# One PSUM tile for each running sum in the gated part, in place of one tile for two

## The chip, the cores and the metric

The kernel runs on one core of a Trainium2 chip. The metric is the device time in microseconds (us) of one execution. The kernel before took 1139.19 us, the median of three runs (1138.51 to 1140.39). One execution was recorded by the profiler; its own time was 1137.8 us, of which the profile shows a span of 1136.0 us.

## The reference

```python
# attention inside chunks of 64 tokens, 8 heads of 64
scores = matmul(q_c, k_c.T) / sqrt(64); attn = softmax(scores); out = matmul(attn, v_c)
x = out as (8*576, 512)
# feed-forward
xn = (x - mean) / sqrt(var + 1e-6) * g_ln
x2 = x + maximum(xn @ w_ch1, 0) @ w_ch2          # 512 -> 2048 -> 512
# gated convolution
gate = sigmoid(causal 5-tap convolution of x2 along the sequence, per channel)
result = (gate * (x2 @ w_val)) @ w_out            # 512 -> 512 -> 512
```

The last line, with its two products of 512x512 weights, is what this text calls the gated part.

## The kernel before

The 4608 tokens are handled as nine blocks of 512. Blocks pass through attention, the feed-forward and the convolution one after the other; the gates of each block and seven prepared operands of its x2 (`x7_dram`) are kept in DRAM. The gated part comes last. For each block it runs a set of seven products for x2 @ w_val (`val`, line 1419) and a set of seven for the product with w_out (`proj`, line 1541). It is the seven-product scheme for 2x2 quadrants, so each product works on quadrants of 256x256. A product is twelve matmuls of 128x256 (`twelve`, line 881, which records all of them at line 888), since each number is carried as a high and a low part.

The seven products carry the names "1" to "7" and add up in two running sums in PSUM, called "a" and "b". Of a set, products 1, 6, 7 and 4 go into a, one upon the other. Products 5 and 3 go into b, and product 2 starts b anew, before 5 in `val` and after 3 in `proj`. Between two products of one sum the sum is read: `shot` (lines 1466 to 1471 in `val`, 1569 to 1573 in `proj`) copies it with ScalarE into SBUF, and `two` (line 1478) or `join` (line 1577) adds it with VectorE to an earlier copy. By these readings the four quadrants arise: c11 from products 1 and 2, c12 from 6 and 3, c22 from 5 and 7, c21 from 4. A product may start only when the reading that its sum is due has been made; so 6 waits for the shot s1 of 1, 7 for the shot u2 of 6, 3 for the shot s5 of 5, and 4 for the join c22 that follows 7.

In `val` the quadrants are multiplied by the gates and split into high and low parts (`split`, tiles `gv`, lines 1489 and 1493), which are the operands of `proj`.

PSUM has eight banks of 128x512 floats. The kernel allocates them under tags: `h0` and `h1` are single banks, `pr`, `yA` and `yB` pairs of banks. A pair is one tile of two banks. Before the gated part `h0`, `h1` hold hidden sums, `yA`, `yB` the feed-forward's results, `pr` the attention. In the gated part the function `banks` (line 1412) hands out the two sums of a set: for `val` of even blocks both banks of `pr` as one tile, for odd blocks `h0` and `h1` as two tiles; for `proj` both banks of `yA` for even and both of `yB` for odd blocks, as one tile each.

The order of the instructions on every engine is made by a list scheduler in the kernel (`Plan.run`, line 53). Each step is an op with an engine, an assumed duration, a list of ops that it depends on, and a priority; `take(tag)` and `hold(tag, ...)` state which earlier ops a room must wait for. The scheduler plays the ops through with its assumed durations and emits them in that order. The semaphore waits are not the scheduler's: the tile layer puts them in afterwards, from the tiles that each emitted instruction reads and writes. Instructions of one engine run in the order in which they were emitted. All DMAs are issued from SP's queue.

Of the kernel before, what the change touches and what calls it, by code (L numbers as in the profile page):

```python
# [31 lines left out]
class Plan:  # L32
# [8 lines left out]
    def add(self, eng, dur, fn, deps=(), pri=0.0):  # L41
        op = Op(eng if isinstance(eng, tuple) else (eng,), dur, fn, deps, pri, len(self.ops))
        self.ops.append(op)
        return op

    def take(self, tag):

        return self.held.get(tag, [])

    def hold(self, tag, *ops):  # L50
        self.held[tag] = list(ops)
# [55 lines left out]
def chunk_attention_ffn_gated_conv(  # L107
# [83 lines left out]
    def bank(tag, name):  # L191
        return psum.tile([P, 512], F32, tag=tag, name=name)

    def pair(tag, name):
        return psum.tile([P, 2, 512], F32, tag=tag, name=name)

    plan = Plan()
    add, take, hold = plan.add, plan.take, plan.hold
# [1206 lines left out]
    def sig_room(i):  # L1405
        if i < 4:
            return qk_room[:, i * 512 : (i + 1) * 512]
        return sums["f32"][:, i - 4]

    V_ORDER, P_ORDER = "2165374", "1657432"  # L1410

    def banks(tag, i):

        if tag == "h":
            return [bank(f"h{x}", f"gp{i}_{x}").rearrange("p (f x) -> p f x", f=2) for x in range(2)]
        t = pair(tag, f"gp{i}")
        return [t[:, x].rearrange("p (f x) -> p f x", f=2) for x in range(2)]

    def val(jj):
        j = TURN[jj]  # L1420
        pri = B0 + SET * jj
        pt = ("pr", "h")[jj % 2]
        pt_free = take("h0") + take("h1") + take("gh") if pt == "h" else take("pr")
        st, xr, sig, sg_op = {}, {}, {}, {}

        def gate(i, kh, h):
            room = 4 * (jj % 2) + i

            def load():
                sig[kh, h] = t = sig_room(room).rearrange("p (k x) -> p k x", k=2)  # L1430
                nc.sync.dma_start(
                    out=t, in_=gate_dram[j][:, 2 * kh : 2 * kh + 2, NB // 2 * h : NB // 2 * (h + 1)]
                )

            def sigmoid():
                nc.scalar.activation(out=sig[kh, h], in_=sig[kh, h], func=AF.Sigmoid)

            stores = [conv_store[j, f] for f in (2 * kh, 2 * kh + 1)]
            first = take("qk") + take("u2") + take("u3") if jj == 0 else []
            ld = add("SP", 1300, load, stores + take(f"sg{room}") + first, pri - SET)  # L1440
            sg_op[kh, h] = add("ACT", 640, sigmoid, [ld, sig_ok], pri - SET / 4)
            return f"sg{room}"

        rooms = {q: gate(i, *q) for i, q in enumerate(((0, 0), (0, 1), (1, 1), (1, 0)))}

        def product(m, into, new, deps):
            rt = X2_RING[x2_n[0] % len(X2_RING)]
            x2_n[0] += 1

            def load():  # L1450
                t = operand(rt[1]) if rt[0] == "o" else slot(rt, [P, 2, 2, 2 * P], F32R, f"x7_{j}_{m}r")
                xr[m] = lambda s, k: t[:, s, k]
                nc.sync.dma_start(out=t.bitcast(F32), in_=x7_dram[j, m].bitcast(F32))

            def go():
                if not st:
                    st["a"], st["b"] = banks(pt, f"v{j}")
                twelve(st[into], wv[m], xr[m], new)

            at = pri + 2 * M_TIME * V_ORDER.index(m)  # L1460
            ld = add("SP", 1300, load, [x7_store[j, m]] + take(rt), at - 30000.0)
            o = add("PE", M_TIME, go, [ld] + wv_op[m] + deps, at)
            hold(rt, o)
            return o

        def shot(into, tag, *deps):
            def go():
                st[tag] = slot(tag, [P, 2, 2 * P], F32, f"v{j}_{tag}")
                nc.scalar.activation(out=st[tag], in_=st[into], func=AF.Copy)

            return add("ACT", 620, go, list(deps) + take(tag), pri - 1e7)

        def two(tag, x, y, op, *deps, rank=-1e7):
            def go():
                if tag not in st:
                    st[tag] = slot(tag, [P, 2, 2 * P], F32, f"v{j}_{tag}")
                a, c = (sig[z] if isinstance(z, tuple) else st[z] for z in (x, y))
                nc.vector.tensor_tensor(out=st[tag], in0=a, in1=c, op=op)

            return add("DVE", 700, go, deps, pri + rank)  # L1480

        def split(m, tag, *deps):
            rt = GV_RING[gv_n[0] % len(GV_RING)]
            gv_n[0] += 1

            def high():
                st[m] = t = slot(rt, [P, 2, 2, 2 * P], F32R, f"gv{j}_{m}")
                gv_o[j, m] = lambda s, k: t[:, s, k]
                nc.scalar.activation(out=t[:, 0], in_=st[tag], func=AF.Copy)

            def low():
                t = st[m]
                nc.vector.tensor_tensor(out=t[:, 1], in0=st[tag], in1=t[:, 0].bitcast(F32), op=ALU.subtract)

            oh = add("ACT", 640, high, list(deps) + take(rt), pri)
            gv_op[j, m] = ol = add("DVE", 700, low, [oh], pri)
            gv_room[j, m] = rt
            return ol

        MUL, ADD, SUB = ALU.mult, ALU.add, ALU.subtract  # L1500
        m2 = product("2", "b", True, pt_free)
        m1 = product("1", "a", True, pt_free)
        s1 = shot("a", "hh0", m1)
        c11 = two("hh0", "hh0", "b", ADD, s1, m2)
        m6 = product("6", "a", False, [m1, s1])
        m5 = product("5", "b", True, [c11])
        u2 = shot("a", "hh1", m6)
        s5 = shot("b", "hl0", m5)
        m3 = product("3", "b", False, [m5, s5])
        m7 = product("7", "a", False, [m6, u2])  # L1510
        c12 = two("hh1", "hh1", "b", ADD, u2, m3)
        c22 = two("hl0", "hl0", "a", ADD, s5, m7)
        m4 = product("4", "a", False, [m7, c22])
        g11 = two("hh0", "hh0", (0, 0), MUL, c11, sg_op[0, 0], rank=-1e5)
        g12 = two("hh1", "hh1", (0, 1), MUL, c12, sg_op[0, 1], rank=-1e5)
        g22 = two("hl0", "hl0", (1, 1), MUL, c22, sg_op[1, 1], rank=-1e5)
        g21 = two("P", "a", (1, 0), MUL, m4, sg_op[1, 0], *take("P"))
        for q, o in (((0, 0), g11), ((0, 1), g12), ((1, 1), g22), ((1, 0), g21)):
            hold(rooms[q], o)
        if pt == "h":  # L1520
            hold("gh", g21, c12)
        else:
            hold("pr", g21, c12)

        l1 = split("1", "hh0", g11)
        s3 = two("hh1", "hh0", "hh1", SUB, g11, g12, rank=0)
        l7 = split("7", "hh1", s3)
        l4 = split("4", "hl0", g22)
        s2 = two("hl0", "hl0", "hh1", SUB, l4, g22, s3, rank=0)
        l6 = split("6", "hl0", s2)  # L1530
        s1_ = two("hh0", "hl0", "hh0", ADD, l1, s2, s3, rank=0)
        l5 = split("5", "hh0", s1_)
        l2 = split("2", "P", g21)
        s4 = two("P", "P", "hl0", SUB, l2, g21, s2, rank=0)
        l3 = split("3", "P", s4)
        hold("hh0", l5)
        hold("hh1", l7, s2)
        hold("hl0", l6, s4, s1_)
        hold("P", l3)

    def proj(jj):
        j = TURN[jj]
        pri = B0 + SET * (jj + 1) + 5 * M_TIME
        pt = f"y{'AB'[jj % 2]}"
        st = {}

        def product(m, into, new, deps):
            def go():
                if "a" not in st:
                    st["a"], st["b"] = banks(pt, f"o{j}")  # L1550
                twelve(st[into], gv_o[j, m], wo[m], new)

            at = pri + 2 * M_TIME * P_ORDER.index(m)
            o = add("PE", M_TIME, go, [gv_op[j, m]] + wo_op[m] + deps, at)
            hold(gv_room[j, m], o)
            return o
# [31 lines left out]
            hold(rooms[h], add("SP", 1300, go, deps, pri))  # L1588

        room0, room1 = (take(r) for r in rooms)  # L1590
        m1 = product("1", "a", True, take(pt))
        s1 = shot("a", 0, 0, m1, *room0)
        m6 = product("6", "a", False, [m1, s1])
        m5 = product("5", "b", True, take(pt))
        u2 = shot("a", 0, 1, m6, *room0)
        s5 = shot("b", 1, 1, m5, *room1)
        m7 = product("7", "a", False, [m6, u2])
# [2 lines left out]
        c21 = shot("a", 1, 0, m4, *room1)  # L1600
        store(1, c21, c22)
        m3 = product("3", "b", False, [m5, s5])
        c12 = join("b", 0, 1, m3, u2)
        m2 = product("2", "b", True, [c12])
        c11 = join("b", 0, 0, m2, s1)
        hold(pt, c21, c11)
        store(0, c11, c12)


# [72 lines left out]
```

## Time and profile before

| what | value |
|---|---|
| median of three runs | 1139.19 us |
| the profiled execution's own time | 1137.8 us |
| its span in the profile | 1136.0 us |
| TensorE matmul busy, over the span | 1092.4 us (96%) |
| TensorE weight loads busy, over the span | 957.0 us (84%) |
| VectorE, ScalarE busy, over the span | 865.3 us (76%), 497.9 us (44%) |
| first product of the gated part | at 921.1 us |
| last matmul ends | at 1130.3 us |

PE stands for TensorE's matmuls, PEld for its weight loads, which run ahead of the matmuls that use them; each matmul has one weight load of its own. DVE is VectorE, ACT ScalarE, SP the queue that issues DMAs. In the trace the `val` sums are `gpv` and the `proj` sums `gpo`; `os` is the SBUF tile that `proj` fills for the output. A number in square brackets at the end of a row of the timeline is the idle time of the engine just before the row, with what ended it.

### The profile page before, as it was taken

Reading aid. Unit: us, or ns where it says so; the run is one execution under the profiler, and the core shown is the slowest. Engines: PE = TensorE matmul, PEld = TensorE weight load, DVE = VectorE, ACT = ScalarE, POOL = GpSimd, SP = SyncE. Lnnn points to the kernel's source line nnn. Section 1 sums busy time; section 2 is a strip of 40 time slices with the busy share of each in tenths; the row PEclk is TensorE's granted clock in tenths of the full one; section 3 lists DMA queues with packets and bytes.
Section 4 is the critical chain, followed back from the end, with each engine's and each line's share of the span. In section 5 each row is a group of like instructions: output and inputs, shape, how many; then the busy total and the mean of one; then the engine's idle time right before and its main releaser. Section 6 shows DMA issues by size and latency. Waiting matters only on the chain.

```text
span 1136.0 us, 22506 instructions
## 1 busy us (share of the span) xinstructions
PE 1092.4 (96%) x8801; PEld 957.0 (84%) x8801; DVE 865.3 (76%) x1537; ACT 497.9 (44%) x893; POOL 29.1 (3%) x78
## 2 busy tenths in 40 slices
PE   5799999999999999999999999999999999999996
PEld 3478888788888888988888888889888888999995
DVE  5889969997867867876786596677748888887654
ACT  5885522334333334433433343343344546554542
POOL 0000000000000000000000000000000000000000
PEclk9889999999999999999999999999999999999999
DMA  9994334765988898888888779789948968999822
GB/s 208 333 290 116 84 98 134 249 211 175 308 255 224 254 328 286 267 296 253 226 276 292 216 219 318 211 228 304 274 147 289 390 235 281 305 316 362 300 77 74
DMA packets 178034, 275.72 MB, mean 243 GB/s; under 512 B 72196, under 2 KB 123400, under 8 KB 177928
## 3 DMA queue, kind: packets, MB, share of 16 engines
q1 hardware_dynamic: 177928, 274.29, 75.8%
q8 instruction: 69, 1.13, 0.4%
q14 instruction: 37, 0.30, 0.1%
HBM read 206.59 MB, written 67.63 MB: 241 GB/s over the span
## 4 chain that ended last, share of the span: by engine, by line
PE 87%; DVE 5%; DMA 3%; SPq 2%; ACT 1%; issue 1%; DVEq 0%; ACTq 0%
PE m L888 23%; PE gpv L888 7%; PE gpo L888 6%; PE yB L1044 5%; PE yA L1044 4%; PE yA L1045 4%; PE yA L1046 4%; PE yB L1045 4%; PE yB L1046 4%; PE att L478 4%; PE att L505 4%; PE h L726 3%; PE y L749 3%; PE h L727 3%; PE h L728 3%; PE y L751 3%
## 5 line engine op out<-in xcount | busy, mean ns | idle before, releaser
L888 PEld LDWEIGHTS m<-late,a 128*128 128x128 f32 x2352 | 298.9, 188 | 18.0 <-ACT c_hl L979 2.0
L888 PE MATMUL m<-late,a 128*128 128x256 f32 x2352 | 308.1, 282 | 3.0 <-ACT c_hl L979 1.1
L1231 DVE SCALAR_TENSOR_TENSOR acc<-X,cw_sb,acc 128x516 f32<-128x516 f32 (+1 forms) x144 | 107.1, 751 | 6.2 <-ACT acc L1224 3.1
L1044 PE MATMUL yB<-h,w 128*128 128x512 f32 x224 | 92.0, 411 | 0.0
L1044 PE MATMUL yA<-h,w 128*128 128x512 f32 x224 | 91.0, 406 | 0.0
L1045 PE MATMUL yA<-h,w 128*128 128x512 f32 x224 | 88.4, 395 | 0.0
L1045 PE MATMUL yB<-h,w 128*128 128x512 f32 x224 | 88.3, 394 | 0.0
L1046 PE MATMUL yA<-h,w 128*128 128x512 f32 x224 | 88.2, 394 | 0.0
L1046 PE MATMUL yB<-h,w 128*128 128x512 f32 x224 | 88.2, 394 | 0.0
L986 DVE TENSOR_TENSOR c_hh<-c_hh,m 128x512 f32<-128x512 f32 x56 | 38.3, 685 | 55.5 <-PE m L888 50.6
L1014 ACT ACTIVATE h<-c_hh 128x512 fp32r<-128x512 f32 x56 | 35.2, 629 | 75.3 <-DVE c_hh L986 75.3
L888 PE MATMUL gpo<-w,gv 128*128 128x256 f32 x432 | 55.5, 283 | 6.3 <-DVE os L1577 6.3
L888 PEld LDWEIGHTS gpo<-w,gv 128*128 128x128 f32 x432 | 52.3, 188 | 8.3 <-DVE os L1577 8.1
L979 ACT ACTIVATE c_hh<-m 128x512 f32<-128x512 f32 x56 | 33.3, 595 | 52.4 <-PE m L888 49.5
L726 PE MATMUL h<-xnt,w 128*128 128x512 f32 x128 | 53.5, 418 | 1.2 <-ACT xnt L608 1.2
L727 PE MATMUL h<-xnt,w 128*128 128x512 f32 x128 | 51.7, 404 | 0.7 <-DVE xnt L612 0.7
L749 PE MATMUL y<-hh,w 128*128 128x512 f32 x128 | 52.3, 408 | 0.0
L728 PE MATMUL h<-xnt,w 128*128 128x512 f32 x128 | 51.4, 402 | 0.0
L751 PE MATMUL y<-hl,w 128*128 128x512 f32 x128 | 50.4, 394 | 0.0
L1046 PEld LDWEIGHTS yB<-h,w 128*128 128x128 f32 x224 | 42.1, 188 | 9.9
L1046 PEld LDWEIGHTS yA<-h,w 128*128 128x128 f32 x224 | 42.1, 188 | 9.8
L750 PE MATMUL y<-hh,w 128*128 128x512 f32 x128 | 50.3, 393 | 0.0
(189 smaller groups left out, 2135.9 us busy)
## 6 DMA issues: line engine op xcount, KB each, us to landing
a<-a SPq DMA_DIRECT2D x196, 512.0 KB, 5.0
x7d<-x SPq DMA_DIRECT2D x63, 512.0 KB, 5.7
raw<-in_moe_w_ch_dram SPq DMA_DIRECT2D x32, 512.0 KB, 8.6
qk_room<-in_q_dram SPq DMA_DIRECT2D x100, 112.0 KB, 4.3
qk_room<-in_k_dram SPq DMA_DIRECT2D x100, 112.0 KB, 4.3
late<-x7d SPq DMA_DIRECT2D x21, 512.0 KB, 5.4
v<-in_v_dram SPq DMA_DIRECT2D x144, 64.0 KB, 3.3
out_dram<-os SPq DMA_DIRECT2D x18, 512.0 KB, 3.9
```

Of the source, the lines that this page charges most:

```text
L478: nc.tensor.transpose(ps[:, c], src[:, c], ident)
L726: nc.tensor.matmul(ps, wh, xh, start=(kk == 0), stop=False)
L727: nc.tensor.matmul(ps, wh, xl, start=False, stop=False)
L728: nc.tensor.matmul(ps, wl, xh, start=False, stop=(kk == KD - 1))
L749: nc.tensor.matmul(ps, wh[:, s], st["hh"], start=opens, stop=False)
L750: nc.tensor.matmul(ps, wl[:, s], st["hh"], start=False, stop=False)
L751: nc.tensor.matmul(ps, wh[:, s], st["hl"], start=False, stop=closes)
L888: nc.tensor.matmul(ps[:, f], l, right(r, k), start=new and f == k == i == 0, stop=k == 1 and i == 2, skip_group_check=True,)
L1044: nc.tensor.matmul(ps, wh, hh, start=opens and f == 0, stop=False)
L1045: nc.tensor.matmul(ps, wl, hh, start=False, stop=False)
L1046: nc.tensor.matmul(ps, wh, hl, start=False, stop=closes and f == 3)
L1231: nc.vector.scalar_tensor_tensor(out=a, in0=X[b][:, f, i : i + L], scalar=cw_sb[:, i, f : f + 1], in1=a, op0=ALU.mult, op1=ALU.add,)
```

## The change

`banks` goes; `half_of` hands out one bank as a tile of its own: `h0` or `h1` whole, or the first bank of a pair, whose second bank then stays unused. In `val` the sum a lives in `h0` for even and `h1` for odd blocks, the sum b always in `pr`. In `proj` a is always in `yA` and b always in `yB`. A sum takes a new tile whenever a product starts it anew, so b takes two tiles in a set. `take` and `hold` now follow each sum separately: the next set's first product into a waits for the last reading of a alone, and that into b for the last reading of b alone. In all, the gated part uses five banks in place of eight.

```diff
-    def banks(tag, i):
-
-        if tag == "h":
-            return [bank(f"h{x}", f"gp{i}_{x}").rearrange("p (f x) -> p f x", f=2) for x in range(2)]
-        t = pair(tag, f"gp{i}")
-        return [t[:, x].rearrange("p (f x) -> p f x", f=2) for x in range(2)]
+    def half_of(tag, name):
+
+        t = bank(tag, name) if tag[0] == "h" else pair(tag, name)[:, 0]
+        return t.rearrange("p (f x) -> p f x", f=2)
 
     def val(jj):
...
-        pt = ("pr", "h")[jj % 2]
-        pt_free = take("h0") + take("h1") + take("gh") if pt == "h" else take("pr")
+        at_bank = {"a": f"h{jj % 2}", "b": "pr"}
...
-                if not st:
-                    st["a"], st["b"] = banks(pt, f"v{j}")
+                if new:
+                    st[into] = half_of(at_bank[into], f"v{j}_{m}")
                 twelve(st[into], wv[m], xr[m], new)
...
-        m2 = product("2", "b", True, pt_free)
-        m1 = product("1", "a", True, pt_free)
+        m2 = product("2", "b", True, take(at_bank["b"]))
+        m1 = product("1", "a", True, take(at_bank["a"]))
...
-        if pt == "h":
-            hold("gh", g21, c12)
-        else:
-            hold("pr", g21, c12)
+        hold(at_bank["a"], g21)
+        hold(at_bank["b"], c12)
...
     def proj(jj):
...
-        pt = f"y{'AB'[jj % 2]}"
...
-                if "a" not in st:
-                    st["a"], st["b"] = banks(pt, f"o{j}")
+                if new:
+                    st[into] = half_of(f"y{into.upper()}", f"o{j}_{m}")
...
-        m1 = product("1", "a", True, take(pt))
+        m1 = product("1", "a", True, take("yA"))
...
-        m5 = product("5", "b", True, take(pt))
+        m5 = product("5", "b", True, take("yB"))
...
-        hold(pt, c21, c11)
+        hold("yA", c21)
+        hold("yB", c11)
```

Since the scheduler sees other dependencies, it emits another order in the gated part. First place: TensorE in the middle of the gated part, where `proj` of block 2 ends beside `val` of block 3. Of each product the first row stands here. `gpo_11278` before, and `o_1_11290` (a) and `o_5_11401` (b) now, are the sums of `proj` of block 2; `gpv_0_11040` and `v_1_11033` are the sum a of `val` of block 3; `v_2_11456` is the sum b of `val` of block 4; `o_1_11528` the sum a of `proj` of block 3; `gv_7`, `gv_3`, `gv_4`, `gv_1`, `gv_2` name the product. Before:

```order
L888 MATMUL gpo_11278<-wo_10663,gv_7_11239 128x256 [waits Activation_49]
...
L888 MATMUL gpo_11278<-w_10562,gv_3_11335 128x256 x2
...
L888 MATMUL gpv_0_11040<-x_3_4r,w_10199 128x256 [waits DMAHW1_49,DVE_49]
...
L888 MATMUL gpo_11278<-w_10426,gv_4_11220 128x256 [waits DVE_49]
...
L888 MATMUL gpv_11298<-late_2904,w_10092 128x256 [waits DMAHW5_49]
...
L888 MATMUL gpo_11278<-w_10562,gv_2_11258 128x256 [waits Activation_49]
```

Now:

```order
L888 MATMUL o_1_11290<-wo_10665,gv_7_11232 128x256 [waits Activation_49]
...
L888 MATMUL v_2_11456<-x_4_2r,w_10199 128x256 [waits DMAHW1_49,DVE_49]
...
L888 MATMUL v_1_11033<-x_3_4r,w_10199 128x256 [waits DMAHW0_49,DVE_49]
...
L888 MATMUL o_1_11290<-w_10426,gv_4_11216 128x256 [waits DVE_49]
...
L888 MATMUL o_5_11401<-w_10563,gv_3_11340 128x256 [waits Activation_49]
...
L888 MATMUL v_1_11548<-x_5_1r,w_10092 128x256 [waits DMAHW3_49,DVE_49]
...
L888 MATMUL o_2_11569<-w_10563,gv_2_11251 128x256 [waits DVE_49]
```

Product 4 stands two products behind 7 in both. Product 3 stood between them and now stands behind 4; product 2 of the next `val` has come between them.

Second place: TensorE at the end of the program, `proj` of block 8, where no `val` is left to stand between; again the first row of each product. Before:

```order
L888 MATMUL gpo_12693<-w_10426,gv_1_12553 128x256 [waits PE_49]
...
L888 MATMUL gpo_12693<-wo_10687,gv_6_12691 128x256 [waits Activation_49]
...
L888 MATMUL gpo_12693<-wo_10693,gv_5_12708 128x256 x2
...
L888 MATMUL gpo_12693<-wo_10663,gv_7_12627 128x256 [waits Activation_49]
...
L888 MATMUL gpo_12693<-w_10562,gv_3_12729 128x256 [waits DVE_49]
...
L888 MATMUL gpo_12693<-w_10426,gv_4_12643 128x256 x3
...
L888 MATMUL gpo_12693<-w_10562,gv_2_12687 128x256 [waits DVE_49]
```

Now:

```order
L888 MATMUL o_1_12728<-w_10426,gv_1_12583 128x256 [waits Activation_49]
...
L888 MATMUL o_5_12747<-wo_10694,gv_5_12724 128x256 [waits DVE_49,Activation_49]
...
L888 MATMUL o_1_12728<-wo_10688,gv_6_12706 128x256 [waits Activation_49]
...
L888 MATMUL o_1_12728<-wo_10665,gv_7_12643 128x256 [waits Activation_49]
...
L888 MATMUL o_5_12747<-w_10563,gv_3_12760 128x256 [waits Activation_49]
...
L888 MATMUL o_1_12728<-w_10426,gv_4_12672 128x256 [waits DVE_49]
...
L888 MATMUL o_2_12816<-w_10563,gv_2_12703 128x256 [waits DVE_49]
```

Products 6 and 5 have changed places, so 5 now stands between 1 and 6, and 7 directly behind 6. The waits of 3 and of 2 name other engines or other counts than before.

Third place: TensorE where the first `proj` begins (`gpo_10774`, now `o_1_10763`), from product 4 of `val` of block 0 on. Before:

```order
L888 MATMUL gpv_10485<-x_0_4r,w_10199 128x256 [waits DMAHW0_49]
...
L888 MATMUL gpv_0_10673<-late_2904,w_10092 128x256 [waits DMAHW2_49]
...
L888 MATMUL gpv_10756<-x_2_2r,w_10199 128x256 [waits DMAHW4_49,DVE_49,PE_49]
...
L888 MATMUL gpo_10774<-w_10426,gv_1_10584 128x256 [waits DVE_49]
...
L888 MATMUL gpv_10756<-x_2_1r,w_10092 128x256 [waits DMAHW0_49]
...
L888 MATMUL gpo_10774<-wo_10687,gv_6_10813 128x256 [waits DVE_49]
```

Now:

```order
L888 MATMUL v_1_10501<-x_0_4r,w_10199 128x256 [waits DMAHW0_49,DVE_49]
...
L888 MATMUL v_2_10738<-late_2904,w_10199 128x256 [waits DVE_49]
...
L888 MATMUL o_1_10763<-w_10426,gv_1_10585 128x256 [waits DVE_49]
...
L888 MATMUL v_1_10785<-x_2_1r,w_10092 128x256 [waits DMAHW0_49,PE_49]
...
L888 MATMUL o_1_10763<-wo_10688,gv_6_10803 128x256 [waits DVE_49]
```

From product 4 of `val` to product 6 of the first `proj` there are now three products (2 of block 1, 1 of the `proj`, 1 of block 2), where there were four.

## Rows read from the trace of the kernel before

**Rows 1.** Busy time by stretch; columns: stretch, its length, each engine busy (instructions), clock, DMA.

```profile
936.00:956.00 20.00, 17.40 (x137) 16.33 (x136) 16.80 (x30) 11.56 (x24) 0.00 (x0) 1.00 0.79 265
956.00:1010.00 54.00, 52.13 (x431) 51.01 (x431) 46.63 (x73) 29.15 (x53) 0.00 (x0) 1.00 0.92 303
1010.00:1070.00 60.00, 58.59 (x491) 57.98 (x491) 42.59 (x67) 31.20 (x56) 0.00 (x0) 1.00 0.97 340
1070.00:1116.00 46.00, 43.59 (x358) 42.44 (x357) 33.10 (x53) 19.97 (x36) 0.00 (x0) 1.00 0.28 99
1116.00:1130.00 14.00, 10.34 (x81) 9.52 (x80) 4.56 (x7) 3.71 (x7) 0.00 (x0) 1.00 0.20 75
```

**Rows 2.** Waits, 936 to 1131 us; columns: who, for whom: us, times, longest.

```profile
PEld gpo L888 <- DVE os L1577: 8.1, 9, 1.6
PEld gpo L888 <- ACT os L1571: 2.1, 3, 1.0
ACT sums L1436 <- DMA sums<-gd: 1.4, 1, 1.4
```

**Rows 3.** Timeline, 1003 to 1009 us; columns: start, length, engine, line, operation.

```profile
1003.63 1.55 PE L888 MATMUL gpo<-wo,gv 128*128 128x256 f32 x12
1005.02 1.60 PE L888 MATMUL gpo<-w,gv 128*128 128x256 f32 x12
1006.46 1.58 PE L888 MATMUL gpv<-x_4r,w 128*128 128x256 f32 x12
1006.72 0.69 DVE L1577 TENSOR_TENSOR os<-os,gpo 128x512 f32<-128x512 f32 x1 [1.27 <-PE gpo L888]
1007.32 0.69 DVE L1478 TENSOR_TENSOR v_hh<-v_hh,v_hh 128x512 f32<-128x512 f32 x1
1007.92 0.68 DVE L1577 TENSOR_TENSOR os<-os,gpo 128x512 f32<-128x512 f32 x1
1008.66 1.48 PEld L888 LDWEIGHTS gpo<-w,gv 128*128 128x128 f32 x12 [0.82 <-DVE os L1577]
```

**Rows 4.** Timeline of the last `proj`, 1117 to 1131 us.

```profile
1117.94 2.89 PEld L888 LDWEIGHTS gpo<-wo,gv 128*128 128x128 f32 x24 [0.99 <-ACT os L1571]
1121.07 0.60 ACT L1571 ACTIVATE os<-gpo 128x512 f32<-128x512 f32 x1 [1.50 <-PE gpo L888]
1121.71 1.47 PEld L888 LDWEIGHTS gpo<-wo,gv 128*128 128x128 f32 x12 [0.89 <-ACT os L1571]
1123.42 0.60 ACT L1571 ACTIVATE os<-gpo 128x512 f32<-128x512 f32 x1 [1.76 <-PE gpo L888]
1124.05 0.69 DVE L1577 TENSOR_TENSOR os<-os,gpo 128x512 f32<-128x512 f32 x1 [3.77 <-ACT os L1571]
1124.79 2.90 PEld L888 LDWEIGHTS gpo<-w,gv 128*128 128x128 f32 x24 [1.61 <-DVE os L1577]
1128.68 1.45 PEld L888 LDWEIGHTS gpo<-w,gv 128*128 128x128 f32 x12 [0.98 <-DVE os L1577]
1130.36 0.60 ACT L1571 ACTIVATE os<-gpo 128x512 f32<-128x512 f32 x1 [6.34 <-PE gpo L888]
1130.99 0.69 DVE L1577 TENSOR_TENSOR os<-os,gpo 128x512 f32<-128x512 f32 x1 [2.36 <-ACT os L1571]
```

**Rows 5.** Timeline where the first `proj` begins, 944 to 955 us.

```profile
946.25 0.69 DVE L1478 TENSOR_TENSOR v_hh<-v_hh,gpv 128x512 f32<-128x512 f32 x1 [1.12 <-PE gpv L888]
947.59 0.68 DVE L1478 TENSOR_TENSOR v_P<-gpv,qk_room 128x512 f32<-128x512 f32 x1
953.80 0.68 DVE L1493 TENSOR_TENSOR gv<-v_hl,gv 128x512 fp32r<-128x512 f32 x1
954.53 0.66 PEld L888 LDWEIGHTS gpo<-wo,gv 128*128 128x128 f32 x5 [0.97 <-DVE gv L1493]
```

**Rows 6.** DMA issues over the program; columns: transfer, queue, count, KB each, median us to landing.

```profile
late<-x7d SPq DMA_DIRECT2D x21, 512.0 KB, 5.4
sums<-gd SPq DMA_DIRECT2D x16, 256.0 KB, 5.8
```

## Prediction

> **What bounds the kernel now.** I read the busy time by stretch first. From 936 us on, when the feed-forward is done, TensorE does nothing but products of the gated part, at a granted clock of 1.00 [rows 1]. What it loses there is what the change can give back. I measure the loss by the weight loads (the second busy column): 194.00 us of stretches hold 177.27 us of them, so 16.7 us are lost: 3.67 in 936 to 956, then 2.99, 2.02 and 3.56 up to 1116 (together 8.57), and 4.48 in the last 14 us [rows 1]. By the matmul column the loss would be 11.95 us. The timeline decides: product 4 of a `proj` starts 2.20 us after the product before it (1006.46 to 1008.66), where an undisturbed one follows after 1.44 (1005.02 to 1006.46). So 0.76 us are lost, and the weight loads show 0.82 [rows 3]. The Trainium skill (Perfetto Trace Analysis, Identifying the Most-Contended Engine) says the same of the two columns: pipelined matmuls look misleading there, and the busy share of LDWEIGHTS is the better measure. By the matmul column the gain below would come out at about 9 us in place of 13.
>
> The list of waits says who is waited for: of the 16.7 us, 8.1 in nine waits end with a join `os` of VectorE, 2.1 with a copy `os` of ScalarE [rows 2].
>
> The timeline shows why these readings are late. Product 7 ends at 1005.18 (1003.63 + 1.55). Its join c22 needs only that and an old copy, and VectorE is idle for 1.27 us, yet c22 starts at 1006.72, right after product 3 has ended (1005.02 + 1.60 = 1006.62) [rows 3]. Product 3 writes the other bank of the same tile. Then product 4, which needs c22 alone (over at 1007.41), starts at 1008.66, when the join of the other bank, c12 (1007.92 + 0.68), is over [rows 3]. Both are waits for the tile, where only a wait for the bank is due. Counted from the semaphore values of the two built programs, 31 of 126 readings of such sums wait for a product that did not write what they read; in the changed program none does.
>
> **The change, part by part.** No instruction is added or removed: the same 126 products, copies and joins. What changes is waits and order. SP issues the same loads and stores; as each load waits for the product that frees its room, they shift with the products, by one or two places, and I cost that at nothing as long as rooms are filled more than the 5.4 us of a landing ahead [rows 6] (if not, see the first rival). One product takes 1.44 us [rows 3], a copy 0.60, a join 0.69 [rows 4], and from the end of one engine's work to the start of the next goes about 0.1 us (1006.62 to 1006.72) [rows 3].
>
> Middle, 956 to 1116 us, 8.57 us lost. I go through a set in the new order and count the products between a reading's source and the product that waits for it. Product 4 of `proj` waits for c22 after 7: two products between (first place of the change), 2.9 us of cover for 0.1 + 0.69 + 0.1. Product 1 of the next set waits for the copy c21 after 4: two between. Product 2 waits for c12 after 3: two. Product 2 of `val`, which now always takes the bank of `pr`, waits for c12 of the set before after 3: three between. The least cover anywhere in a middle set is one product, 1.44 us, against 0.8 us of copy and hops. So no wait of this kind should be left. Below nothing it cannot go; what may stay are small queues on VectorE and ScalarE. I leave 0.4 us. As upper bound I take 0.27 us a set, 1.9 us, a third of the 0.82 seen now [rows 3]. Gain 8.2.
>
> Start, 936 to 956 us, 3.67 us lost. Here the chain on VectorE binds: from the gating of product 4 (947.59) to the low part of operand 6 (953.80 + 0.68) go 6.9 us, and product 6 of the first `proj` waits for that with 0.97 us lost [rows 5]. VectorE is busy for 16.80 of these 20 us [rows 1], and none of this work goes away. But c12 now need not wait for product 4, as it did (1.12 us idle, 946.25) [rows 5]; product 4 ended about 0.1 before that, at 946.1. So the gating of 4 can start at about 946.5 and operand 6 is ready at 953.4. TensorE has three products and a sixth of one between (third place of the change): 946.1 + 4.3 + 0.2 = 950.6, so 2.8 us are lost, plus perhaps 0.2 elsewhere: 3.0 in place of 3.67. Bounds: 2.1, if the splitting of the w_out sums lets operand 6 through earlier by as much as one product less, and 4.2, if a load is late there as well: product 1 of block 2 stands about 5 us behind the end of the product that frees its room, loads land in 5.4 us in the median [rows 6]; but that wait lies beside the one for operand 6.
>
> End, 1116 to 1130 us, 4.48 us lost in four waits [rows 4]. The 0.99 before product 6 (copy s1 after 1) goes, since 5 stands between now. The 1.61 before 3 goes: 3 writes b and needs the copy s5 of 5, which did not start until 7 was over (1123.42), and then a join of a (1124.05) that is none of its business. The 0.98 before 2 goes: c12 needs 3, and 4 stands between. The 0.89 before 7 stays: now 7 stands directly behind 6, so copy and hops are bare. With 0.1 for operand 5, 1.0 us stays, and 3.5 are gained.
>
> After the last matmul the last join (1130.99) starts only behind the last copy (1130.36), though it reads the other bank [rows 4]. Now c21 is read a product earlier, and the join can start where the copy did: 0.6 us gained. Queue, store and end stay.
>
> Sum: 0.7 + 8.2 + 3.5 + 0.6 = 13.0 us. From 1137.8 us of the profiled execution that gives 1124.8; the median of the runs lies 1.4 us above that execution, so 1126.2 us. With the best bounds (2.1, 0 and 0.9 left) the gain is 14.3, with the worst of these (4.2, 1.9, 1.3) 9.9.
>
> **The rivals.**
>
> *The transfers hold it.* From 956 to 1070 the DMA engines are busy for 0.92 to 0.97 of the time, at 303 to 340 GB/s [rows 1]. If they cannot deliver faster, the loss up to 1070 stays as other waits, and only that behind it goes: 3.56 less 0.1, 3.5 and 0.6, in all 7.6, which gives 1131.6. Against it: 340 GB/s in one stretch are more than 303 in the other, so 303 is not the limit, and loads land in 5.4 us though rooms are filled one and a half sets ahead [rows 6].
>
> *VectorE is next.* It is busy for 46.63 of 54 us in 956 to 1010 [rows 1]. If its queue makes c22 and c12 late by itself, half of the middle loss stays: 13.0 - 4.3 = 8.7, 1130.5. Against it: joins follow each other every 0.60 us though each is shown with 0.69 [rows 3], so the true load is an eighth less.
>
> *Five banks are too few (slower).* Each sum now has one bank for all sets, and the next set's first product must wait for the last reading. For product 1 of `proj` that is c21, a copy on ScalarE with two products of cover, 2.9 us. ScalarE runs in order, and the sigmoids stand in its queue; before one of them it waited 1.4 us for its gate load [rows 2], and gate loads land in 5.8 us [rows 6]. If a gate comes 3.0 us late in each set, c21 ends 3.0 + 1.3 (two copies or splits queued before it) + 0.6 after product 4, and TensorE loses 2.0 us in each of eight sets: 16.5 us against the 13.0 gained, 1142.7 with the end. It decides from 1.6 us a set. The Trainium skill speaks for this one (Perfetto Trace Analysis, Matmul Optimizations): all eight PSUM banks should be used, for parallelism. No row here shows what the three banks left unused would be worth.
>
> *It does nothing:* other waits of the same length take the place, 1139.
>
> **How the numbers follow.** The forecast has 0.70, its own range is 1124 to 1129.5. The transfers have 0.12, VectorE 0.09, nothing 0.05, too few banks 0.04. The range that should hold the time 8 times in 10 is 1123.8 to 1132.0: it takes in the first two rivals. A measurement of this kernel tells a change from none at about 0.2%, 2.3 us. Faster by more: 0.70 + 0.12 + 0.09 = 0.91; within: 0.05; slower: 0.04.
>
> **What would show it.** In the profile after, the waits of the weight loads for a join `os` should fall from 8.1 us to under 1. c22 should start within 0.2 us of the end of product 7, if VectorE is free, and a product of another sum should stand behind it without idle time. The weight loads should fill all but about 4.5 us from 936 us to the last matmul, 3 of them before 956. In the last set one wait of about 0.9 us should be left, before product 7, and the last join should start within 0.2 us of the last matmul's end. I am wrong if waits for a copy c21 or for the bank of `pr` show in every set, if loads `x` or gates land in more than 8 us and are waited for, or if VectorE shows joins that start late without waiting for anything.

## The result and the profile after

| | before | after |
|---|---|---|
| median of the runs | 1138.85 us (4 runs, 1137.84 to 1140.39) | 1123.65 us (4 runs, 1122.15 to 1127.80) |
| the profiled execution's own time, its span | 1137.8, 1136.0 us | 1127.8, 1126.0 us |
| last matmul begins | 1130.05 us | 1121.24 us |

The changed kernel takes 0.9871 of the time before, with a 95% interval of 0.9843 to 0.99: faster by 14.7 us (11 to 18). 1126.2 were predicted; the time lies 0.15 us below the low end of the range (1123.8 to 1132.0). The profiled execution of after is the slowest of its four, and one stretch of it tells why (below).

Busy time by stretch, with the columns of [rows 1]; before, the weight loads filled 16.33, 51.01, 57.98 and 42.44 us of the first four:

```profile
936.00:956.00 20.00, 17.16 (x124) 15.80 (x123) 17.06 (x30) 10.72 (x24) 0.00 (x0) 0.94 0.76 247
956.00:1010.00 54.00, 54.00 (x443) 54.00 (x443) 48.31 (x74) 30.53 (x54) 0.00 (x0) 0.96 0.91 308
1010.00:1070.00 60.00, 60.00 (x511) 60.00 (x510) 47.18 (x74) 34.18 (x60) 0.00 (x0) 1.00 0.98 353
1070.00:1116.00 46.00, 45.31 (x382) 45.11 (x381) 31.73 (x50) 21.77 (x38) 0.00 (x0) 1.00 0.30 107
```

From 956 us on TensorE stands still once, for 0.89 us. The waits of the weight loads after, 936 us to the end, answer to [rows 2]:

```profile
PEld v L888 <- issue: 2.1, 1, 2.1
PEld o L888 <- DVE gv L1490: 1.3, 2, 0.8
PEld o L888 <- ACT os L1565: 0.9, 1, 0.9
PEld o L888 <- ACT gv L1486: 0.3, 1, 0.3
```

The join `os` of VectorE, 8.1 us before, is gone from the list. What is left lies at the start, but for the copy `os` in the last set. A middle set after, where product 7 is followed by its join c22 and by product 4, answers to [rows 3] (the sums are now named `v` and `o`):

```profile
1005.63 1.55 PE L888 MATMUL o<-wo,gv 128*128 128x256 f32 x12
1007.01 1.59 PE L888 MATMUL v<-x_2r,w 128*128 128x256 f32 x12
1007.37 0.68 DVE L1571 TENSOR_TENSOR os<-os,o 128x512 f32<-128x512 f32 x1
1008.44 1.58 PE L888 MATMUL v<-x_4r,w 128*128 128x256 f32 x12
1009.75 3.36 PEld L888 LDWEIGHTS o<-w,gv 128*128 128x128 f32 x28
```

Product 7 ends at 1007.18 (1005.63 + 1.55), c22 starts 0.19 us later, two products of `val` stand behind it, and product 4 starts without idle time. Before, c22 started 1.54 us after product 7. The last set, which answers to [rows 4]:

```profile
1115.65 1.47 PEld L888 LDWEIGHTS o<-wo,gv 128*128 128x128 f32 x12 [0.89 <-ACT os L1565]
1117.17 4.35 PE L888 MATMUL o<-w,gv 128*128 128x256 f32 x36
1120.19 0.60 ACT L1565 ACTIVATE os<-o 128x512 f32<-128x512 f32 x1 [4.10 <-PE o L888]
1121.56 0.69 DVE L1571 TENSOR_TENSOR os<-os,o 128x512 f32<-128x512 f32 x1 [2.10 <-PE o L888]
```

One wait of 0.89 us is left, before product 7, and the last join starts 0.04 us after the last matmul's end (1121.52). The two last stores, before and then after (columns as in the timeline, SPq is the queue that issues):

```profile
1130.98 1.09 SPq L1584 DMA_DIRECT2D out_dram<-os  x2
```

```profile
1120.81 1.83 SPq L1578 DMA_DIRECT2D out_dram<-os  x2
```

Before, both halves of the last block left together, right at the end. Now the first leaves at 1120.81, while TensorE still works, and the second follows 1.46 us behind it (1122.27), in place of 0.72 (1131.70). The last four stores land in 2.8 us in the median, in place of 3.2. From the start of the last matmul to the end of the span it is 4.76 us (1126.0 - 1121.24) in place of 5.95 (1136.0 - 1130.05).

The start, which answers to [rows 5], and below it the windows around it:

```profile
948.83 1.26 PEld L888 LDWEIGHTS o<-w,gv 128*128 128x128 f32 x10 [0.54 <-DVE gv L1490]
950.84 0.63 ACT L1433 ACTIVATE qk_room<-qk_room 128x512 f32<-128x512 f32 x1 [1.91 <-DMA qk_room<-gd]
952.02 0.69 DVE L1490 TENSOR_TENSOR gv<-v_hh,gv 128x512 fp32r<-128x512 f32 x1 [1.38 <-ACT gv L1486]
952.23 1.47 PEld L888 LDWEIGHTS v<-x_1r,w 128*128 128x128 f32 x12 [2.14 <-issue]
954.04 0.50 PEld L888 LDWEIGHTS o<-wo,gv 128*128 128x128 f32 x2 [0.35 <-ACT gv L1486]
955.30 2.21 PEld L888 LDWEIGHTS o<-wo,gv 128*128 128x128 f32 x10 [0.77 <-DVE gv L1490]
```

```profile
952.00:956.00 4.00, 3.19 (x17) 2.66 (x18) 3.94 (x7) 2.90 (x6) 0.00 (x0) 0.71 1.11 368
956.00:960.00 4.00, 4.00 (x21) 4.00 (x21) 3.42 (x6) 2.12 (x4) 0.00 (x0) 0.50 0.71 275
```

TensorE waits 3.80 us here in four pieces; the longest, 2.14 us, is for the load `x` of product 1 of block 2. Then the granted clock falls to 0.50, the lower of its two levels (1.2 GHz): only 21 matmuls run in 4 us. In the profile before the clock stayed at 1.00 here.

### The profile page after: what moved, and what is told of

Same layout as the page of the kernel before. It is cut to its first block, busy times and chain, and to the rows that moved or that the text cites. A ratio compares the mean times of both kernels' runs of the same rounds, so it can differ in the third digit from the quotient of the medians.

```text
span 1126.0 us, 22527 instructions
## 1 busy us (share of the span) xinstructions
PE 1090.5 (97%) x8801; PEld 958.8 (85%) x8801; DVE 866.4 (77%) x1537; ACT 498.8 (44%) x893; POOL 29.1 (3%) x78
## 4 chain that ended last, share of the span: by engine, by line
PE 86%; DMA 7%; DVE 3%; SPq 2%; issue 1%; ACT 1%; ACTq 0%; DVEq 0%
PE m L888 22%; PE o L888 8%; PE v L888 7%; PE yB L1044 4%; PE yA L1044 4%; PE yB L1045 4%; PE yB L1046 4%; PE yA L1045 4%; PE yA L1046 4%; PE att L478 4%; PE att L505 3%; PE h L726 3%; PE y L749 3%; PE h L727 3%; PE h L728 3%; PE y L751 3%
## 5 line engine op out<-in xcount | busy, mean ns | idle before, releaser
L888 PE MATMUL o<-w,gv 128*128 128x256 f32 x432 | 53.7, 281 | 0.3 <-DVE gv L1490 0.3
L888 PEld LDWEIGHTS o<-w,gv 128*128 128x128 f32 x432 | 52.0, 188 | 0.5 <-DVE gv L1490 0.5
```

The costliest lines, as they stand in the source:

```text
L888: nc.tensor.matmul(ps[:, f], l, right(r, k), start=new and f == k == i == 0, stop=k == 1 and i == 2, skip_group_check=True,)
```

## The experiments

Times of single parts are below what whole runs resolve, so I divide TensorE's gated work by counting matmuls from the last one back. Every kernel here has the same 8801 in its record. "Start" runs from the 1600th to the 1350th last (917.38 to 956.58 us before), "middle" to the 100th (1113.70), "end" to the last (1130.05). Undisturbed, the 1250 matmuls of the middle take 147.6 us, 0.118 each.

| kernel | order | `val` tiles | `proj` tiles | median, us | ratio to before (95%) | start | middle | end |
|---|---|---|---|---|---|---|---|---|
| before | old | shared | shared | 1138.85 | 1 | 39.20 | 157.13 | 16.34 |
| pairs_new_order | new | shared | shared | 1137.40 | 0.9987 (0.9974 to 1.0) | 40.63 | 151.39 | 18.39 |
| pairs_proj | new | own | shared | 1131.17 | 0.9932 (0.992 to 0.9944) | 39.02 | 148.19 | 18.30 |
| old_order_proj | old | shared | own | 1129.77 | 0.9927 (0.9905 to 0.9949) | 39.23 | 152.00 | 13.22 |
| pairs_val | new | shared | own | 1127.86 | 0.991 (0.9896 to 0.9924) | 40.62 | 150.42 | 12.59 |
| after | new | own | own | 1123.65 | 0.9871 (0.9843 to 0.99) | 41.84 | 147.61 | 12.59 |
| after_again | new | own | own | 1123.23 | 0.9866 (0.9849 to 0.9884) | 39.26 | 147.56 | 12.58 |

The change has two parts: the tiles, and the order that the planner makes once each sum's room is followed apart. The first four experiments separate them.

**The new order with the old tiles.** The edit, in `val` and the same in `proj`, with `banks` put back:

```diff
-                if new:
-                    st[into] = half_of(at_bank[into], f"v{j}_{m}")
+                if not st:
+                    st["a"], st["b"] = banks(("pr", "h")[jj % 2], f"v{j}")
```

> The changed kernel's order of instructions on every engine, but the tiles of the kernel before: both sums of a proj set are one tile of a pair, and both sums of a val set of an even block too. Theory 1 (the tile that two sums share makes a reading wait for a product that did not write what it reads): all of the gain is lost again, time 1136 to 1142 us, 13 to 18 above the changed kernel, and waits of the weight loads for joins `os` are back, 6 us or more. Theory 2 (the new order, which follows each sum's room apart, brings the gain): time stays within 3 us of the changed kernel. Theory 3 (half and half): about 1131.

Measured: 1137.40 us, against 1138.87 for the kernel before beside it. The gain is gone but for 1.5 us (0 to 3.0), as theory 1 has it; theory 2 falls, for the time as a whole. The five longest groups among the waits of its weight loads, 936 to 1131 us:

```profile
PEld gpo L888 <- ACT os L1572: 4.3, 4, 1.6
PEld gpo L888 <- DVE gv L1497: 2.8, 2, 1.9
PEld gpo L888 <- DVE os L1578: 2.4, 4, 1.0
PEld gpv L888 <- ACT v_hl L1473: 1.4, 3, 0.5
PEld gpv L888 <- DVE v_hh L1482: 1.4, 2, 0.9
```

But one detail of theory 1 is wrong too: the joins `os` are back with 2.4 us only, not 6 or more. By stretches, the new order with shared tiles saves 5.7 us of the middle (157.13 to 151.39), and gives 2.1 back at the end and 1.4 at the start.

**Shared tiles in `val` alone, and in `proj` alone** (one half of the edit above each).

> The changed kernel's order, but the two sums of a val set of an even block are one tile again (pair pr); proj keeps a tile for each sum. Theory 1: only the waits of val come back. Of the 8.57 us lost in the middle before, some 5.7 were waits of proj, so val is worth 2 to 3 us: time 1 to 4 us above the changed kernel. Theory 2: the same time as the changed kernel.

> The changed kernel's order, but the two sums of a proj set are one tile again (pairs yA, yB in turn); val keeps a tile for each sum. Theory 1: the waits of proj come back, 5.7 us in the middle, 3.5 at the end and 0.6 before the last join: time 9 to 13 us above the changed kernel, and with the val kernel's loss it adds up to that of the kernel with both. Theory 2: the same time as the changed kernel.

Measured against the changed kernel's 1123.23 us on the same chip: 4.6 us more with `val` shared, 7.9 with `proj` shared, 14.2 with both. Both sizes were expected somewhat wrongly: `val` is worth more than the 1 to 4 us expected, `proj` less than the 9 to 13. The two add up to 12.6 us, which these few runs can't tell from 14.2. The stretches say where. A shared `val` costs 2.9 us of the middle (150.42) and 1.4 of the start; a shared `proj` costs 5.7 of the end (18.30), 1.2 behind the last matmul and only 0.6 of the middle (148.19). In the profile with `proj` shared the waits for `os` are the same two groups as with both shared, 4.3 and 2.4 us (above), and 6.3 of these 6.7 us come after 1108 us, where no products of `val` are left to stand between two of `proj`.

**The old order with a tile for each sum of `proj`** (`val` as before). Its edit is to the kernel before:

```diff
-                if "a" not in st:
-                    st["a"], st["b"] = banks(pt, f"o{j}")
+                if new:
+                    st[into] = half_of(f"y{into.upper()}", f"o{j}_{m}")
```

> The order of the kernel before on every engine, its val unchanged, but in proj a tile for each sum, a in yA and b in yB: the proj half of the change in tiles without the change in order. Theory 1 (shared tiles alone make the waits): the waits of weight loads for joins `os` fall from 8.1 us to 2 or less, and 6 to 9 us are gained on the kernel before (1130 to 1133 us). Theory 2 (the wait for the tile and the order are two covers for the same loss: in the middle sets the new order hides what the shared tile costs, as the kernel with shared proj tiles in the new order lost only 0.6 us there): in the old order, too, the tiles alone take most of the middle's proj waits away, 5 to 6 us, but of the end's 4.5 us less than 2, as product 6 still stands right behind 1; 1131 to 1134 us. Theory 3 (tiles without the new order bring nothing): within 2 us of the kernel before.

Measured: 1129.77 us, 8.3 (0.0073 of 1138.24; interval 5.8 to 10.8) less than before. Theory 1 holds here with its 6 to 9 us: the joins `os` vanish from the waits, whole, and copies `os` are left:

```profile
PEld o L888 <- ACT os L1576: 3.1, 5, 0.9
```

The middle gains 5.1 us (157.13 to 152.00), and the end 3.1, more than theory 2 left it; its 1131 to 1134 us were too many as well. What theory 2 says of the middle holds: the new order alone takes 5.7 us off it, own tiles in `proj` alone 5.1, and the two together (`pairs_val`) 6.7, not 10.8. They are in large part covers for the same loss; own tiles in `val` bring it to 9.6. At the end they are not: there the new order by itself costs 2.1 us, own tiles by themselves save 3.1, and both save 3.8. The corner that is missing, the old order with own tiles in `val`, can't be made with these five tags: a new sum would need the bank of `pr` while the one before it is still to be read (in the old order product 2 of block 2 stands directly behind product 1 of block 1, as the third place of the change shows).

**The changed kernel again.**

> The changed kernel again, unaltered, for its time beside the three others and a second profile. Time 1122 to 1125 us. If the fall of the granted clock to 0.5 at 956 to 960 us follows from the TensorE idle time just before it (2.1 us for a load and 1.7 us more), it is there again, and the profiled time is again about 1127; if it was chance of one execution, the clock stays above 0.9 there and the profiled time is 1122 to 1124.

```profile
947.45 2.50 PEld L888 LDWEIGHTS v<-x_1r,w 128*128 128x128 f32 x12 [1.65 <-issue]
950.54 1.46 PEld L888 LDWEIGHTS o<-wo,gv 128*128 128x128 f32 x10 [0.17 <-DVE gv L1490]
```

```profile
944.00:948.00 4.00, 2.20 (x15) 1.81 (x15) 3.10 (x7) 2.28 (x5) 0.00 (x0) 0.95 0.95 350
948.00:952.00 4.00, 4.00 (x23) 3.83 (x23) 3.96 (x7) 3.18 (x6) 0.00 (x0) 0.62 1.11 365
```

The clock falls again, but for a shorter time and earlier, so that product 1 of block 2 runs slowly (2.50 us of weight loads in place of 1.47) beside the wait for operand 6: the start takes 39.26 us, not 41.84. This profiled execution took 1120.88 us, the first one 1127.8; of the 6.9 us between them 2.6 are the start and 4.3 the stages before it (the 1600th last matmul begins at 914.92 and at 919.20), which the change does not touch. The median is 1123.23 us, as expected; of the two cases for the clock neither is met as it stands.

**What bounds the start: a sigmoid that waits for its gate, or a late load.** In the changed kernel's rows of the start, ScalarE waits 1.91 us for the gate load of a sigmoid at 950.84, and VectorE then 1.38 us for the split queued behind it. The first edit makes the planner place such sigmoids later:

```diff
+                    if op.seq in self.slow:
+                        wait = 6000.0
...
+            if jj < 3:
+                plan.slow.add(ld.seq)
```

> The changed kernel, but the planner reckons with 6.0 us in place of 3.5 from the issue of a gate load of the first three blocks to its landing, so that ScalarE gets those sigmoids up to three places later; the order on TensorE is the same. Theory A (the start is bound by the chain on VectorE and ScalarE up to operand 6, in which a sigmoid that waits 1.9 us for its gate holds up the split behind it): operand 6 comes 1 to 1.5 us earlier, and so much is gained from the first product of the gated part to its last. Theory B (the start is bound by the late load of product 1 of block 2, 1.7 to 2.1 us waited): the wait for that load stays and under 0.5 us is gained.

The second gives product 1 of block 2 the room of product 6, which comes free earlier:

```diff
-            rt = X2_RING[x2_n[0] % len(X2_RING)]
+            turn = {"1": 1, "6": -1}.get(m, 0) if jj == 2 else 0
+            rt = X2_RING[(x2_n[0] + turn) % len(X2_RING)]
```

> The changed kernel, but products 1 and 6 of block 2 exchange their rooms, so that the load for product 1 is issued two products (some 2.8 us) earlier; product 1 moves one place ahead on TensorE with it. Theory B (the late load bounds the start): its wait of 1.7 to 2.1 us goes or falls below 0.5, and 1.5 to 2 us are gained from the first product of the gated part to its last. Theory A (the chain up to operand 6 bounds it): the wait for the load goes, but the wait before product 6 grows by as much, gain under 0.5 us. If the fall of the granted clock at this place comes with the wait for that load, it is gone in both cases, and that gives 1 to 3 us more against executions that had it.

The later sigmoids first, then the exchanged rooms, in their weight loads:

```profile
952.50 1.47 PEld L890 LDWEIGHTS v<-x_1r,w 128*128 128x128 f32 x12 [1.54 <-issue]
954.96 1.25 PEld L890 LDWEIGHTS o<-wo,gv 128*128 128x128 f32 x10 [0.74 <-DVE gv L1494]
```

```profile
950.97 0.30 PEld L888 LDWEIGHTS o<-wo,gv 128*128 128x128 f32 x2 [2.71 <-ACT gv L1487]
952.24 2.21 PEld L888 LDWEIGHTS o<-wo,gv 128*128 128x128 f32 x10 [0.97 <-DVE gv L1491]
```

With the rooms exchanged the wait for the load is gone, and the wait for operand 6 has grown to 2.71 us. Counted from the 1600th last matmul, product 6 goes on at 35.65 us (952.24 - 916.59); in the kernel with the new last order below, whose start is that of the changed kernel, it does so at 35.68 (955.28 - 919.60). So the load was no bound, and theory A holds: the chain up to operand 6 is. The later sigmoids bring that point to 34.88 us (954.96 - 920.08), 0.8 earlier; the start takes 38.35 us, 0.8 less than in that kernel (39.15), a little under the 1 to 1.5 expected, and the wait for the load stays, at 1.54. Its time, 1122.83 us (ratio 0.9865, 0.9842 to 0.9889), can't be told from the changed kernel's.

With the rooms exchanged the kernel came out some 4 us slower than the changed one, at 1127.25 us (0.9906, 0.9882 to 0.993; the intervals overlap a little). The windows of the exchanged rooms, and a wait that this order has in the middle:

```profile
948.00:952.00 4.00, 1.07 (x6) 0.56 (x5) 3.03 (x6) 3.03 (x6) 0.00 (x0) 0.90 1.06 381
952.00:956.00 4.00, 3.76 (x17) 3.76 (x18) 3.42 (x7) 2.92 (x6) 0.00 (x0) 0.50 1.03 368
```

```profile
1033.11 1.48 PEld L888 LDWEIGHTS o<-wo,gv 128*128 128x128 f32 x12 [0.67 <-ACT os L1566]
```

My expectation that the fall of the clock would go with the load's wait was wrong: it came here behind a gap that had another cause. The start takes 41.66 us with the waits in one piece of 2.71 us, against 39.15 in the kernel with the new last order, which has them apart and kept its clock; the changed kernel's first profile, where the clock fell, has 41.84. The middle takes 148.32 us, 0.8 more than the changed kernel's, most of it the wait shown.

**The wait left at the end.** Product 7 of the last set stands right behind 6 and waits for the copy u2 between them. The edit puts 3 ahead of 7:

```diff
-        m7 = product("7", "a", False, [m6, u2])
+        m3 = product("3", "b", False, [m5, s5]) if end else None
+        m7 = product("7", "a", False, [m6, u2, m3])
```

> The changed kernel, but in the last proj set product 3 goes ahead of 7 (and 2 ahead of 4), so that another product covers the copy u2 between 6 and 7. Expected by the mechanism of cover: the one wait left at the end, 0.89 us before product 7, goes, and no other comes: 0.9 us less from the middle to the end. Rival: operand 3, the last to be split, is late, or the last reading is now the copy of c21 with its store behind it; then nothing is gained.

```profile
1112.67 1.08 ACT L1565 ACTIVATE os<-o 128x512 f32<-128x512 f32 x2 [1.73 <-PE o L888]
1113.81 1.47 PEld L888 LDWEIGHTS o<-w,gv 128*128 128x128 f32 x12 [1.38 <-ACT os L1565]
```

It failed: the wait grew to 1.38 us and the end to 13.07 (1124.66 us, 0.9875, 0.9852 to 0.9897). Neither the rival's late operand nor its last copy did it. Product 3 needs the copy s5 of product 5, which stands behind u2 in ScalarE's order, since the planner holds s5 back until its output room is free. Both copies run after product 6 (x2, 1.08 us).

**Four banks.**

```diff
-        at_bank = {"a": f"h{jj % 2}", "b": "pr"}
+        at_bank = {"a": "h0", "b": "pr"}
```

> The changed kernel, but the sum a of val is in h0 for all blocks in place of h0 and h1 in turn: four banks, one for each of the four sums, which is the least that this scheme can do with. The planner makes its order anew from that. Theory 1 (a bank counts only by the cover between the last reading of a sum and the next product into it; between product 4 of a val set and product 1 of the next stand products of the proj set): the middle stays without waits and the time within 2 us of the changed kernel; at the start, where val sets follow each other without a proj set between, up to 2 us more may be lost. Rival (the number of banks in use is what counts, and the step from eight to five already cost something that the gain hides): the step from five to four loses 5 us or more, in waits of weight loads for the gating of product 4 in every set.

```profile
952.23 0.50 PEld L888 LDWEIGHTS o<-wo,gv 128*128 128x128 f32 x2 [3.70 <-ACT gv L1486]
952.96 2.21 PEld L888 LDWEIGHTS o<-wo,gv 128*128 128x128 f32 x10 [0.23 <-DVE gv L1490]
```

1127.03 us (0.9909, 0.9879 to 0.9939), but the middle takes 147.69 us and the end 12.58: no wait in either. All of the loss that the profile shows is at the start (41.11), where one product less is at hand before operand 6 and the clock falls behind the gap (0.57 from 952 to 956). So theory 1 holds for the middle and for the 2 us at the start, and the rival's waits in every set are not there. The median, 3.4 to 3.8 us above the changed kernel's, is more than the 2 us that theory 1 allowed; the profile does not show where the rest would be, and these six executions differ by 10 us among themselves.

**A version that takes what these showed:** the later sigmoids, the new last order, and output rooms for the last set that are free early.

```diff
+            if jj == NBLK - 1:
+                rooms.append([r for r in X2_RING if r[0] != "o"][h])
+                continue
```

> The changed kernel with the later sigmoids of the first three blocks, and in the last proj set product 3 ahead of 7 and 2 ahead of 4, this time with output rooms of its own for that set, so that the copy s5 no longer stands behind the copy u2 in ScalarE's queue. If the wait of 1.38 us in the kernel with the last order alone came from that queue, no wait of the weight loads over 0.2 us is left in the last set, and the stretch from the 100th last matmul to the last takes 11.7 us in place of 12.6. If the cover of one product is too short by itself, a wait of 0.5 us or more stays. In all 0.5 to 2 us less than the changed kernel: 1121.5 to 1123 us.

```profile
PEld o L890 <- DVE gv L1494: 1.5, 2, 0.9
PEld v L890 <- issue: 1.4, 1, 1.4
```

```profile
1109.87 0.60 ACT L1572 ACTIVATE os<-o 128x512 f32<-128x512 f32 x1 [0.30 <-PE o L890]
1110.98 1.48 PEld L890 LDWEIGHTS o<-w,gv 128*128 128x128 f32 x12
1111.30 0.60 ACT L1572 ACTIVATE os<-o 128x512 f32<-128x512 f32 x1 [0.83 <-PE o L890]
1112.39 1.47 PEld L890 LDWEIGHTS o<-wo,gv 128*128 128x128 f32 x12
```

The copy s5 now runs right after 5, and no wait is left in the last set: the end takes 11.65 us, as expected. Start, middle and end make 197.6 us, against 199.4 in the better of the changed kernel's two profiles and 212.7 before. 1122.1 us, ratio 0.9857 (0.9835 to 0.9879): the lowest time here, though runs alone don't separate it from the changed kernel.

## Why the prediction was right, and where it was not

**The mechanism** is the one predicted, with one addition. Tiles that two sums share made readings wait for a product that writes the other bank; with the new order kept and only the tiles put back, the gain is gone. What I did not see is that in the middle the order covers such waits as well. I credited the whole 8.2 us to the tiles; the runs show 5.1 for own tiles in `proj` in the old order, 5.7 for the order with shared tiles, 6.7 for these two together, and 9.6 once `val` has its own tiles too.

**Middle, gain 8.2 forecast, 9.6 measured** (157.13 - 147.56). The 0.4 us that I left for small queues did not occur. The other 1.0 is in the measure: the weight loads show 8.57 us lost [rows 1], but from the start of one matmul to the next the same stretch loses 9.6. By the matmuls' busy time it would be 5.7 (160 less 52.13, 58.59 and 43.59) [rows 1]. The Trainium skill (Perfetto Trace Analysis, Identifying the Most-Contended Engine) prefers the weight loads to the matmuls as a measure. The trace agrees with it, and the starts of the matmuls are nearer still.

**End, 3.5 forecast, 3.8 measured** (16.34 - 12.58), and the wait of 0.89 us left is the one named, before product 7.

**Last join, 0.6 forecast,** starts where it was expected. But "queue, store and end stay" was wrong: the copy c21 now comes early enough for the first of the two last stores to go ahead, so from the last matmul on 1.2 us are gained (5.95 - 4.76). The kernels with own tiles in `proj` and this end unaltered show it in either order (4.8), both with shared ones in the new order don't (some 6.0).

**Start, 0.7 forecast: this step failed.** Operand 6 did come 1.1 us earlier, as worked out: product 6 goes on 36.10 us after the 1600th last matmul (955.30 - 919.20) in place of 37.15 (954.53 - 917.38). But I let product 4 of block 0 end as late as before, at 946.1. Its weight loads, before and then after:

```profile
940.02 1.48 PEld L888 LDWEIGHTS gpv<-x_7r,wv_sums 128*128 128x128 f32 x12 [0.89 <-ACT v_hh L1469]
943.12 1.47 PEld L888 LDWEIGHTS gpv<-x_3r,w 128*128 128x128 f32 x12 [0.20 <-DVE v_hl L1478]
944.52 1.48 PEld L888 LDWEIGHTS gpv<-x_4r,w 128*128 128x128 f32 x12
```

```profile
945.15 1.49 PEld L888 LDWEIGHTS v<-x_4r,w 128*128 128x128 f32 x12
```

It came 1.2 us earlier too (25.95 us after the 1600th last matmul in place of 27.14), since the waits of 0.89 and 0.20 us ahead of it went as well, and TensorE waited that much longer at operand 6. One product fewer stands ahead of that point, as I had counted: 222 matmuls from the 1600th on, in place of 234. With product 4 ending 1.1 us earlier, my sum for that wait would have given 3.9 us in place of 2.8. So 3.8 us were lost in place of 3.0 (3.6 in the kernel with the new last order, which has the same start), inside the bounds of 2.1 to 4.2, and the start gained nothing where the clock held (39.15 us with the new last order, 39.20 before). I had named the late load of product 1 of block 2 and said that it lies beside the wait for operand 6; the exchange of rooms shows that this was so. What I had not reckoned with is the clock: the first profiled execution, where it fell, took 2.7 us longer for the start than the kernel with the new last order (41.84 - 39.15), which has the same start and kept its clock.

**The sum:** 0 + 9.6 + 3.8 + 1.2 = 14.6 us in place of 13.0, and the runs say 14.7 (11 to 18). The rivals fall: DMA engines move 353 GB/s from 1010 to 1070 us without a wait of TensorE; VectorE's 48.31 of 54 us hold up nothing; and the sums' banks are never waited for. Behind that last one I had set a rule of the Trainium skill (Perfetto Trace Analysis, Matmul Optimizations): use all eight PSUM banks, for parallelism. Here five banks lose nothing in the middle, and four hardly more (147.69 us), and the measurement decides: there a wait for a tile, not the number of banks, was the limit. At the start four banks do cost a product of cover (41.11 us), and what own tiles in all eight banks would do there no run shows. In that rival's sum, eight sets of 2.0 us make 16.0, not the 16.5 that I wrote. ScalarE did wait for gates, as that rival feared; it cost something at the start alone.

## What to carry to other kernels

A tile of several banks is waited for as a whole; give each sum that is written and read by itself a tile of its own, and count the products between a reading and the one that needs it, not the banks. To value such a change, cross its two halves, the tiles and the order that comes with them: here either alone would have looked like the cause of the middle's loss. Where an engine must wait for several things in a row, find the last one before moving another: the load that was waited for longest was worth nothing.

## What the hardware did that was not expected

The granted clock fell to 0.50 after gaps at the start in four of the twelve profiled executions: longest wait 2.14 us (0.50 from 956 to 960), 1.65 (a mean of 0.62 from 948 to 952), 2.71 (0.50 from 952 to 956) and 3.70 (a mean of 0.57 from 952 to 956). It stayed at 1.00 with a longest wait of 1.73 in the kernel with the new last order and of 1.86 with `val` shared:

```profile
948.00:952.00 4.00, 2.54 (x21) 2.54 (x22) 4.00 (x9) 3.04 (x6) 0.00 (x0) 1.00 0.99 351
952.00:956.00 4.00, 2.35 (x17) 1.94 (x16) 3.97 (x7) 3.25 (x6) 0.00 (x0) 1.00 1.09 371
```

There TensorE was about as idle in all (its weight loads fill 4.5 of 8 us) as in the first profile of after (4.2), with a shorter longest wait. The length of one wait does not decide it alone (1.65 with a fall, 1.73 and 1.86 without), nor does the sum of them: waits of 0.54, 1.65 and 0.17 us came with a fall in the second profile of after, waits of 1.86, 1.09 and 0.97 here without. What does stays open, as does what share of the executions that were only timed had such a fall.
